# A low-rank mixer on Trainium2: the token mixing from tile 104 on in whole PSUM banks, from a second copy of V

## The chip, the core and the metric

The kernel runs on one core of one Trainium2 chip. Its engines are TensorE (PE in the profile; PEld is its weight loads), VectorE (DVE), ScalarE (ACT), GpSimd (POOL) and SyncE (SP), which issues DMA transfers. The metric is the device time of one execution in microseconds (us). Three runs of the kernel before gave 324.23, 324.48 and 324.81, median 324.48.

## What is computed

```python
def _attn_ref(x, weight):                 # x: (8, 4224, 192), weight: (8, 7)
    w = softmax of weight over its 7 taps
    x_pad = 6 zero rows ahead of x along seq
    out[b, s, head h] = sum_k w[h, k] * x_pad[b, s + k, head h]
    return out                            # a causal convolution, 8 heads of 24

def _moe_ref(x, U, V, w_ch1, w_ch2):      # x is the convolution's result, y below
    xt = x.transpose(0, 2, 1)
    h = xt @ U @ V                        # U: (4224, 32), V: (32, 4224)
    u = x + h.transpose(0, 2, 1)
    ch = np.maximum(u @ w_ch1, 0.0) @ w_ch2   # 192 -> 768 -> 192
    return (u + ch).astype(np.float32)
```

## The kernel before

**Tiles.** A tile is 128 tokens; each of the 8 batches has NT = 33 tiles, 264 in all. Eight tiles make a group, 33 groups. A batch goes through: load of x (four DMA issues on GpSimd's queue, f32 to bf16), GpSimd copies of x shifted by blocks (`x_shift`, six steps), convolution as matmuls with band matrices (`conv32`, L349) evicted by ACT and VectorE into `yt[b]`, then tt = Uᵀy (`tt_mm`, L412; `tt_split`, L426 and L427), the sum of its four partial results with a matrix R (`tt_sum`, L438), which leaves `ttb[b]` with the same 32 rows on all four quarters of the partitions.

**h and u.** `h_tiles(b, j0, j1)` makes h for tiles j0 to j1 of a batch: one matmul for each tile (L469; weights: 32 rows of V by 128 tokens, moving operand: 32 rows of ttb by 192 columns). The PE array is used as four row tiles of 32 rows. Two neighbouring tiles, a pair, share a PSUM bank (384 of its 512 columns), and pair pr uses row tile pr mod 4, so that `V_sb` holds on each quarter of the partitions only the tiles of its pairs. VectorE then adds y to h out of PSUM into the group's buffer `u_sb` (L492), one instruction for a pair, or two where the pair crosses a block of four tiles. A finished group is transposed by a DMA on SP's queue (`transp`, L513, `uT<-u_sb`).

**The channel part.** `w1(g)` (L589) multiplies uT by W1: 36 matmuls of 512 columns, two at a time on two row tiles of 64 rows, with relu evictions by ACT (L603) and VectorE (L605); VectorE takes five of a group's twelve. `w2(g, t0, 2)` (L616) multiplies by W2 for two tiles, 12 matmuls of 192 columns on the whole array; VectorE adds u (L625) and SP's queue stores the result (L633).

**The order** is written out by hand. `SLOTS` lists steps: each has groups for `w1`, then groups for `w2`, and a table that says what is inserted ahead of which of the `w2` pieces (position 0 is ahead of the first, and directly behind W1). Slots 5 to 13 have three groups each: slot k runs groups 3k-9 to 3k-7, so slot 6 runs 9, 10 and 11, and slot 13 the last three. The entries: `c4:0:2:A` is the convolution of batch 4 for 2 heads from head 0 on, with the pattern of engines that evict it; `x5:4` four steps of the shift for batch 5; `t4` tt of batch 4, `s4` its sum; `w105:117` h for tiles 105 to 116 and the transposes of the groups that end there. h runs ahead of W1: in slot 6, tiles 105 to 128 are made while W1 and W2 of tiles 72 to 95 run.

**Buffers.** All PSUM tiles come in turn from one pool of 8 banks, so a matmul that opens a bank waits until the bank of eight allocations before is evicted. `ys` has 3 buffers, `us` 7, `uts` 5, `outs` 8.

**Loads.** `LOADS` ties the four loads of x for a batch to W1's groups: they are held until a named matmul of W1 is done. x of batch 4 is loaded during W1 of groups 6 and 7, in slot 5.

Of the kernel before, what the change touches and what calls it, by code (L numbers as in the profile page):

```python
# [7 lines left out]
ALU = mybir.AluOpType  # L8
ACT = mybir.ActivationFunctionType
BF16 = mybir.dt.bfloat16  # L10
# [4 lines left out]
def kernel(  # L15
# [10 lines left out]
    nc = tc.nc  # L26
    P = nc.NUM_PARTITIONS
    B, S, D = x.shape
# [4 lines left out]
    NT = S // P  # L33
# [3 lines left out]
    NTT = B * NT  # L37
    NG = NTT // GT
    assert NG * GT == NTT
    HB = P // 2  # L40
# [9 lines left out]
    uts = ctx.enter_context(tc.tile_pool(name="uts", bufs=5))  # L50
    rls = ctx.enter_context(tc.tile_pool(name="rls", bufs=3))
    outs = ctx.enter_context(tc.tile_pool(name="outs", bufs=8))
    sml = ctx.enter_context(tc.tile_pool(name="sml", bufs=2))
    psp = ctx.enter_context(tc.tile_pool(name="psp", bufs=8, space=bass.MemoryType.PSUM))

    def bank():
        return psp.tile([P, 512], F32, name="ps", tag="ps")
# [5 lines left out]
    yt = [None] * B  # L63
# [39 lines left out]
    def iota(t, pattern, base, mul):  # L103
# [20 lines left out]
        out=Ur[:, 0:nfull, :], in_=U4[0 : nfull * P, :].rearrange("(k p) c -> p k c", p=P)  # L124
# [10 lines left out]
    for q in range(4):  # L135
        src = moe_V[:, 0 : full * 8 * P].rearrange("r (k q t) -> r k q t", q=4, t=2 * P)
        nc.gpsimd.dma_start(
            out=V_sb[32 * q : 32 * q + 32, 0 : 2 * full, :].rearrange(
                "r (k a) t -> r k (a t)", a=2
            ),  # L140
            in_=src[:, :, q, :],
        )
    W1_sb = cst.tile([P, 3, M4], BF16, name="W1_sb")
    for hf in range(2):
        nc.gpsimd.dma_start(
            out=W1_sb[HB * hf : HB * hf + HB, :, :],
            in_=moe_w_ch1[:, :].rearrange("(c k) m -> k c m", k=HB),
# [6 lines left out]
    for r in range(4):  # L154
        nc.vector.memset(rq[QB * r : QB * r + QB, 0:1], float(QB * r))
    nc.vector.tensor_scalar(
        out=rq[:, 1:2], in0=rq[:, 0:1], scalar1=-4.0, scalar2=None, op0=ALU.mult
# [19 lines left out]
    for hh in range(2):  # L177
# [3 lines left out]
        out=dif[:], in0=dif[:], scalar1=rq[:, 0:1], scalar2=None, op0=ALU.add  # L181
# [5 lines left out]
        out=d_sb[:],  # L187
        in0=w_sb[:],
        in1=mx_sb[:].unsqueeze(2).to_broadcast([P, H, KC]),
        op=ALU.subtract,  # L190
# [5 lines left out]
        out=hot[:],  # L196
        in0=dif[:].unsqueeze(1).to_broadcast([P, KC, BW]),
        in1=tap[:].unsqueeze(2).to_broadcast([P, KC, BW]),
        op=ALU.is_equal,
# [3 lines left out]
        out=ident[:], in0=fp[:], scalar1=float(P), scalar2=None, op0=ALU.is_equal  # L203
# [9 lines left out]
        out=c_sb[:].rearrange("p k h -> p h k"),  # L213
        in0=e_sb[:],
        in1=rs_sb[:].unsqueeze(2).to_broadcast([P, H, KC]),
        op=ALU.mult,
    )
    prs = []
    for hh in range(2):
# [3 lines left out]
            out=pr[:],  # L223
            in0=hot[:].unsqueeze(2).to_broadcast([P, KC, HQ, BW]),
            in1=c_sb[:, :, HQ * hh : HQ * hh + HQ].unsqueeze(3).to_broadcast([P, KC, HQ, BW]),
            op=ALU.mult,
# [5 lines left out]
        out=Eq[:], in0=efp[:], scalar1=rq[:, 1:2], scalar2=None, op0=ALU.is_equal  # L232
# [3 lines left out]
        out=fp[:], in0=fp[:], scalar1=R - 1, scalar2=None, op0=ALU.bitwise_and  # L236
# [3 lines left out]
        out=R4[:], in0=fp[:], scalar1=0.0, scalar2=None, op0=ALU.is_equal  # L240
# [163 lines left out]
    ttb = [[] for _ in range(B)]  # L404
# [46 lines left out]
    def u_group(g):  # L451
        if ut[g] is None:
            ut[g] = us.tile([P, 4, 3, 2, HB], BF16, name="u_sb")
        return ut[g]
# [46 lines left out]
    def h_span(t0, t1):  # L501
        while t0 < t1:
            b = t0 // NT
            te = min(t1, (b + 1) * NT)
            h_tiles(b, t0 - b * NT, te - b * NT)
            t0 = te

    def h_group(g):
        h_span(g * GT, g * GT + GT)

    def transp(g):
        uTt[g] = uts.tile([P, 4, 3, P], BF16, name="uT")
        return nc.sync.dma_start_transpose(  # L513
            out=uTt[g][:].rearrange("p i c t -> p (i c) t"),
            in_=ut[g][:].rearrange("p i c f k -> p (i c f k)"),
        )
# [118 lines left out]
    def held(ins, after):  # L635
        tc.add_manual_dep(
            ins.ins,
            after.ins.name,
            mybir.DependencyInfo(mybir.DependencyClass.Sync, mybir.DependencyReason.DATA),
            reason="transfer held back",  # L640
        )

    def x_load(b, q, after):
        if q == 0:
            x_tile(b)
            x_zero(b, nc.gpsimd)
        held(x_part(b, *XP[q]), after)
# [25 lines left out]
            },  # L673
        ),
    ]
    spans = {
        5: [(80, 88), (88, 96), (96, 105)],
        6: [(105, 117), (117, 129)],
        7: [(129, 140), (140, 152)],
        8: [(152, 164), (164, 175)],  # L680
        9: [(175, 187), (187, 198)],
        10: [(198, 210), (210, 222)],
        11: [(222, 233), (233, 245)],
        12: [(245, 253), (253, 264)],
        13: [],
    }
    for k in range(5, 14):
        gs = list(range(3 * k - 9, 3 * k - 6))
        hs = [f"w{t0}:{t1}" for t0, t1 in spans[k]]
        if k == 5:  # L690
            at = {
                2: ["c3:0:3:AAD"],
                3: ["c3:3:3:AAD"],
                4: ["c3:6:2:A", "x4:4"],
                5: [hs[0]],
                6: ["t3"],
                8: ["s3", hs[1]],
                11: [hs[2]],
            }
        elif k < 10:  # L700
            b = k - 2
            at = {
                0: [f"c{b}:0:2:AAD"],
                2: [f"c{b}:2:3:A"],
                4: [f"c{b}:5:3:AD"] + ([f"x{b + 1}:4"] if b + 1 < B else []),
                5: [hs[0]],
                9: [f"t{b}", hs[1]],
                12: [f"s{b}"],
            }
        elif k < 13:  # L710
            at = {0 if k == 12 else 2: [hs[0]], 5 if k == 12 else 7: [hs[1]]}
        else:
            at = {}
        SLOTS.append((gs, gs, at))

    LOADS = {3: [(4, 1), (4, 4), (5, 1), (5, 4)]}
    for b in range(4, B):
        g = 3 * b - 6
# [26 lines left out]
    for r, (k0, k1) in KP[2].items():  # L745
        j = NB0 // 2 * r + k0
        nc.gpsimd.tensor_copy(
            out=U4_sb[:, o : o + k1 - k0, :, :],
            in_=U_sb[:]
# [8 lines left out]
        out=V_sb[0:32, 2 * (NT // 8), :], in_=moe_V[:, (NT - 1) * P : NT * P]  # L758
# [35 lines left out]
    for r in range(4):  # L794
        q = slice(QB * r, QB * r + QB)
        for hh in range(2):
            nc.gpsimd.tensor_copy(
                out=band2[q, HQ * hh : HQ * hh + HQ, :],
                in_=bands[hh][q, :, HB * (r % 2) : HB * (r % 2) + QB],
            )  # L800

    def do(what):
        if what[0] == "c":
            b, h0, n, engs = what[1:].split(":")
            conv32(int(b), int(h0), int(n), engs)
            return
        if what[0] == "d":
            for h in range(H):
                last = conv(int(what[1:]), h, 1, [0, 1], "AA" if h == 2 else "AD")
            held(transp(3), last)  # L810
            done.append(last)
            return
        if what[0] == "l":
            b, q = (int(v) for v in what[1:].split(":"))
            x_load(b, q, done[-1])
            return
        if what[0] == "x":
            b, n = (int(v) for v in what[1:].split(":"))
            if not steps:
                steps.extend(x_shift(b))  # L820
            for _ in range(n):
                steps.pop(0)()
            return
        if what[0] == "w":
            t0, t1 = (int(v) for v in what[1:].split(":"))
            h_span(t0, t1)
            for g in range(t0 // GT, t1 // GT):
                transp(g)
            return
        n = int(what[1:])  # L830
        if what[0] == "h":
            h_group(n)
            if n > 1 and n != 3:
                transp(n)
        elif what[0] == "t":
            tt_split(n, tt_mm(n, range(NT)))
        else:
            tt_sum(n)

    for gs1, gs2, at in SLOTS:  # L840
        for g in gs1:
            ends = w1(g, RELU0 if g == 1 else RELU)
            for b, blocks in LOADS.items():
                for q, (gb, m) in enumerate(blocks):
                    if gb == g:
                        x_load(b, q, ends[m])
                        if steps:
                            steps.pop(0)()
            if g == 0:
                do("h2")  # L850
        while steps and gs1 != [3]:
            steps.pop(0)()
        npc = 4 * len(gs2)
        for p in range(npc + 1):
            for what in at.get(p, []):
                do(what)
            if p < npc:
                g, k = gs2[p // 4], p % 4
                if g == NG - 1 and k == 3:
                    w2(g, 6, 1)  # L860
                    w2(g, 7, 1)
                else:
                    w2(g, 2 * k, 2)
# [30 lines left out]
```

## Time and profile before

| | |
|---|---|
| median of three runs | 324.48 us |
| the profiled execution | 323.12 us, of which its span is 321.3 us |
| granted TensorE clock | full over the whole span |
| W1, L589: 1188 matmuls | 131.5 us busy |
| W2, L616: 1584 matmuls | 139.8 us busy |
| h, L469: 264 matmuls | 12.0 us busy |
| convolution, L349: 384 matmuls | two groups of 11.8 us busy that lie on each other |
| h + y, L492 on VectorE: 96 of 384 columns, 72 of 192 | 48.4 and 22.4 us busy; 547 and 347 ns each |
| relu, L605 on VectorE: 163 | 105.7 us busy, 688 ns each |
| relu, L603 on ACT: 233 | 124.3 us busy, 604 ns each |
| W2 + u, L625 on VectorE: 131 of 384 columns | 68.8 us busy, 553 ns each |
| DMA queue 1 (stores, transposes) | 38.08 MB, 46.0% of 16 engines' span |
| DMA queue 0 (loads by GpSimd) | 14.60 MB, 39.6% |
| transposes, L513 | 31, from issue to landing 3.2 / 3.8 / 7.9 us (least, median, most) |

A slot of the middle takes 27.8 us. Times of matmuls in the groups are those of one instruction from its start to its modelled end, and they overlap; what a piece of TensorE's work takes is read from the chain of waits, where each row gives start, length, engine, line and count.

### The profile page before, as it was taken

Reading aid. Unit: us, or ns where it says so; the run is one execution under the profiler, and the core shown is the slowest. Engines: PE = TensorE matmul, PEld = TensorE weight load, DVE = VectorE, ACT = ScalarE, POOL = GpSimd, SP = SyncE. Lnnn points to the kernel's source line nnn. Section 1 sums busy time; section 2 is a strip of 40 time slices with the busy share of each in tenths; the row PEclk is TensorE's granted clock in tenths of the full one; section 3 lists DMA queues with packets and bytes.
Section 4 is the critical chain, followed back from the end, with each engine's and each line's share of the span. In section 5 each row is a group of like instructions: output and inputs, shape, how many; then the busy total and the mean of one; then the engine's idle time right before and its main releaser. Section 6 shows DMA issues by size and latency. Waiting matters only on the chain.

```text
span 321.3 us, 9597 instructions
## 1 busy us (share of the span) xinstructions
PE 314.9 (98%) x4004; PEld 218.7 (68%) x4004; DVE 268.7 (84%) x550; ACT 169.5 (53%) x344; POOL 141.6 (44%) x108
## 2 busy tenths in 40 slices
PE   7999999999999999999999999999999999999996
PEld 3757576478677647946864884686597497487495
DVE  6779989987977986996998699699898888897864
ACT  1766723960874396088249609824904903912910
POOL 8763199529947982993798398000000000000000
PEclk9999999999999999999999999999999999999999
DMA  9999993998997999799799963169077079059035
GB/s 105 191 195 169 196 232 101 196 190 253 210 165 147 263 153 194 189 201 154 191 241 139 191 185 111 52 179 218 2 215 228 3 169 275 2 171 272 2 109 188
DMA packets 122443, 53.39 MB, mean 166 GB/s; under 512 B 87712, under 2 KB 122400, under 8 KB 122400
## 3 DMA queue, kind: packets, MB, share of 16 engines
q1 hardware_dynamic: 84528, 38.08, 46.0%
q0 software_dynamic: 37728, 14.60, 39.6%
q8 instruction: 31, 0.51, 0.7%
q14 instruction: 12, 0.10, 0.1%
q10 hardware_dynamic: 144, 0.10, 0.1%
HBM read 29.22 MB, written 25.95 MB: 172 GB/s over the span
## 4 chain that ended last, share of the span: by engine, by line
PE 91%; ACT 3%; DMA 2%; DVE 2%; POOL 1%; issue 1%; POOLq 0%
PE ps L616 42%; PE ps L589 39%; PE ps L349 3%; PE ps L469 3%; DMA x_sb<-in_x_dram 2%; PE ps L412 2%; ACT rl_sb L603 2%; ACT y_sb L266 1%; PE ps L379 1%; POOL x_sb L79 1%; DVE u_sb L492 1%; DVE rl_sb L605 1%; PE ps L438 0%; PE ps L536 0%; DVE out_sb L625 0%
## 5 line engine op out<-in xcount | busy, mean ns | idle before, releaser
L603 ACT ACTIVATE rl_sb<-ps 128x512 bf16<-128x512 f32 x233 | 124.3, 604 | 89.1 <-PE ps L589 77.6
L616 PE MATMUL ps<-W_sb,rl_sb 128*128 128x192 bf16 x1584 | 139.8, 246 | 0.2
L616 PEld LDWEIGHTS <-rl_sb 128*128 128x128 bf16 x1584 | 128.4, 98 | 12.2 <-issue 11.9
L589 PE MATMUL ps<-uT,W_sb 64*128 64x512 bf16 x1188 | 131.5, 376 | 0.3 <-DVE uT L268 0.2
L605 DVE TENSOR_SCALAR rl_sb<-ps 128x512 bf16<-128x512 f32 x163 | 105.7, 688 | 15.2 <-PE ps L589 14.9
L589 PEld LDWEIGHTS <-W_sb 64*128 64x128 bf16 x1188 | 61.3, 94 | 65.9 <-issue 3.0
L625 DVE TENSOR_TENSOR out_sb<-ps,u_sb 128x384 f32<-128x384 f32 (+1 forms) x133 | 69.5, 550 | 25.9 <-PE ps L616 25.0
L315 POOL COPY xb_sb<-x_sb 32x3072 bf16<-32x3072 bf16 (+1 forms) x24 | 67.7, 2820 | 1.1
L492 DVE TENSOR_TENSOR u_sb<-y_sb,ps 128x192 bf16<-128x192 bf16 (+1 forms) x168 | 65.8, 461 | 0.0
L303 POOL COPY xb_sb<-x_sb 128x3072 bf16<-128x3072 bf16 x12 | 32.9, 2742 | 41.5 <-PE ps L349 33.8
L266 ACT ACTIVATE y_sb<-ps 128x408 bf16<-128x408 f32 (+4 forms) x90 | 38.2, 519 | 11.9 <-PE ps L349 9.8
L79 POOL DMA_DIRECT2D x_sb<-in_x_dram x32 | 27.1, 852 | 12.5 <-PE ps L469 7.7
L268 DVE CAST y_sb<-ps 128x408 bf16<-128x408 f32 (+4 forms) x36 | 19.2, 578 | 1.3 <-PE ps L379 1.2
L426 ACT ACTIVATE tt_hi<-ps 128x192 bf16<-128x192 f32 x8 | 2.6, 330 | 27.4 <-PE ps L412 27.4
L469 PE MATMUL ps<-tt_sb,V_sb 32*128 32x192 bf16 x264 | 12.0, 245 | 0.0
L349 PE MATMUL ps<-x_sb,band 64*32 64x384 bf16 x192 | 11.8, 332 | 0.0
L349 PE MATMUL ps<-xb_sb,band 64*32 64x384 bf16 x192 | 11.8, 331 | 0.0
L469 PEld LDWEIGHTS <-V_sb 32*128 32x128 bf16 x264 | 5.8, 92 | 5.7 <-issue 5.5
L379 PE MATMUL ps<-x_sb,band 64*64 64x240 bf16 (+3 forms) x192 | 8.0, 276 | 0.4 <-DMA x_sb<-in_x_dram 0.3
L379 PEld LDWEIGHTS <-band 64*64 64x64 bf16 x192 | 6.0, 106 | 2.2 <-issue 1.5
L349 PEld LDWEIGHTS <-band 64*32 64x32 bf16 x384 | 4.3, 89 | 4.7 <-issue 2.4
L412 PE MATMUL ps<-y_sb,U_sb 128*32 128x192 bf16 x258 | 7.4, 247 | 0.0
(65 smaller groups left out, 66.5 us busy)
## 6 DMA issues: line engine op xcount, KB each, us to landing
out_dram<-out_sb SPq DMA_DIRECT2D x131, 192.0 KB, 3.0
x_sb<-in_x_dram POOLq DMA_DIRECT2D x14, 384.0 KB, 7.2
x_sb<-in_x_dram POOLq DMA_DIRECT2D x7, 432.0 KB, 7.8
x_sb<-in_x_dram POOLq DMA_DIRECT2D x7, 408.0 KB, 7.2
W_sb<-in_moe_w_ch_dram POOLq DMA_DIRECT2D x3, 288.0 KB, 7.5
x_sb<-in_x_dram POOLq DMA_DIRECT2D x1, 504.0 KB, 7.4
uT<-u_sb SPq DMA_TRANSPOSE x31, 3.8
x_sb<-in_x_dram POOLq DMA_DIRECT2D x1, 480.0 KB, 5.6
```

The source lines that it names most:

```text
L79: return nc.gpsimd.dma_start(out=xt[b][HB * r : HB * r + HB, s0:s1, :], in_=x[b, blk * HB : (blk + s1 - s0) * HB, :].rearrange("(j p) d -> ...
L266: nc.scalar.activation(out=out, in_=in_, func=ACT.Copy)
L303: nc.gpsimd.tensor_copy(out=xbt[b][:, s0:s1, :], in_=xt[b][:, s0 + 1 : s1 + 1, :])
L315: nc.gpsimd.tensor_copy(out=xbt[b][q, s0:s1, :], in_=xt[b][q, s0:s1, :])
L349: nc.tensor.matmul(out=pp[r][QB * cg : QB * cg + QB, 0 : nk[r] * GS], lhsT=w[hr], rhs=t[hr, st : st + 2 * nk[r] - 1 : 2, hs], start=True, ...
L469: last = nc.tensor.matmul(out=banks[pr][:, a * D : (a + 1) * D], lhsT=V_sb[32 * q : 32 * q + 32, (j // 8) * 2 + j % 2, :], rhs=ttb[b][32 * ...
L492: nc.vector.tensor_tensor(out=u_group(g)[:, i : i + n, :, hf, :], in0=yt[b][:, run[0] : run[0] + n, :].rearrange("p n (c k) -> p n c k", c=3),
L589: last = nc.tensor.matmul(out=pps[m][hf][:], lhsT=W1_sb[HB * hf : HB * hf + HB, c, m * P : (m + 1) * P], rhs=uTt[g][HB * hf : HB * hf + HB ...
L603: nc.scalar.activation(out=rl[:, m, hf, :], in_=pp[hf][:], func=ACT.Relu)
L605: nc.vector.tensor_scalar_max(out=rl[:, m, hf, :], in0=pp[hf][:], scalar1=0.0)
L616: last = nc.tensor.matmul(out=cps[:, a * D : (a + 1) * D], lhsT=rlt[g][:, m, hf, (i + a) * P : (i + a + 1) * P], rhs=W2_sb[:, m, :], start ...
L625: nc.vector.tensor_tensor(out=o[:, 0:n, :].rearrange("p n (c k) -> p n c k", c=3), in0=cps[:, 0 : n * D].rearrange("p (n c k) -> p n c k", ...
```

## The change

h from tile 104 on is cut in chunks of 64 columns, three to a tile, and eight chunks fill a PSUM bank (512 columns). `h_banks(n)` makes the next n banks, up to four at a time, one on each row tile; a tile that lies across two banks takes two matmuls, with the tile's V as weights in both. Since any row tile may now need any tile of V, `V4_sb` holds all of V on each quarter of the partitions. It is loaded by four issues on GpSimd's queue (`v4_load`) behind W1 of group 7, after the loads of x for batch 4. Its pool stands behind the other large pools, and its rows have 64 unused columns, 896 bytes in all. Tiles below 104 are made as before.

The hand-written order of slots 5 to 12 changes too: h comes as `b4` and `b6` (four and six banks), the convolution's pieces of batches 5 to 7 stand closer together with other engine patterns, and tt and its sum are made at other places: t4 at position 5 of slot 6 and s4 at position 11, t5 in slot 8 between two pieces of the convolution and s5 at position 5, t6 and t7 at position 5 of slot 9.

```diff
+    vs = ctx.enter_context(tc.tile_pool(name="vs", bufs=1))
...
+    TH0 = 104
+    NCH = 3 * TH0
+    VC = 3
+    V4_sb = vs.tile([P, NT // VC, VC * P + HB], BF16, name="V4_sb")
+
+    def v4_load():
+        for q in range(4):
+            nc.gpsimd.dma_start(
+                out=V4_sb[32 * q : 32 * q + 32, :, 0 : VC * P],
+                in_=moe_V[:, :].rearrange("r (j t) -> r j t", t=VC * P),
+            )
+
+    made = [0]
+
+    def h_banks(n):
+
+        c0 = NCH + 8 * made[0]
+        made[0] += n
+        c1 = c0 + 8 * n
+        assert c1 <= 3 * NTT
+        for s0 in range(c0, c1, 32):
+            ps, todo = [], []
+            for k in range(s0, min(s0 + 32, c1), 8):
+                p, q, parts = bank(), len(ps), []
+                for t in range(k // 3, (k + 7) // 3 + 1):
+                    a, e = max(k, 3 * t), min(k + 8, 3 * t + 3)
+                    parts.append((p, q, k, t, a, e))
+                ps.append((p, k))
+                todo.append(parts)
+            for n in range(max(len(parts) for parts in todo)):
+                for parts in todo:
+                    if n >= len(parts):
+                        continue
+                    p, q, k, t, a, e = parts[n]
+                    nc.tensor.matmul(
+                        out=p[:, HB * (a - k) : HB * (e - k)],
+                        lhsT=V4_sb[
+                            32 * q : 32 * q + 32,
+                            t % NT // VC,
+                            t % VC * P : t % VC * P + P,
+                        ],
+                        rhs=ttb[t // NT][
+                            32 * q : 32 * q + 32, HB * (a - 3 * t) : HB * (e - 3 * t)
+                        ],
+                        start=True,
+                        stop=True,
+                        tile_position=(32 * q, 0),
+                    )
+            for p, k in ps:
+                a = k
+                while a < k + 8:
+                    b, blk = a // (3 * NT), a // 12
+                    e = min(k + 8, 12 * (blk + 1), 3 * NT * (b + 1))
+                    y0, i0 = a - 3 * NT * b, a - 12 * blk
+                    nc.vector.tensor_tensor(
+                        out=u_group(blk // 2)[:].rearrange("p i c f k -> p (i c) f k")[
+                            :, i0 : i0 + e - a, blk % 2, :
+                        ],
+                        in0=yt[b][:].rearrange("p j (c k) -> p (j c) k", c=3)[
+                            :, y0 : y0 + e - a, :
+                        ],
+                        in1=p[:, HB * (a - k) : HB * (e - k)].rearrange(
+                            "p (n k) -> p n k", k=HB
+                        ),
+                        op=ALU.add,
+                    )
+                    a = e
+        for g in range(c0 // 24, c1 // 24):
+            transp(g)
+
...
-    spans = {
-        5: [(80, 88), (88, 96), (96, 105)],
-        6: [(105, 117), (117, 129)],
...
-        12: [(245, 253), (253, 264)],
-        13: [],
+    late_slots = {
+        5: "2:c3:0:3:AAD 3:c3:3:3:AAD 4:c3:6:2:A 4:x4:4 5:w80:88 6:t3 8:s3 8:w88:96 11:w96:104",
+        6: "0:c4:0:2:A 2:c4:2:3:AAD 4:c4:5:3:AAD 4:x5:4 5:b4 5:t4 8:b4 11:s4",
+        7: "0:c5:0:2:AD 1:c5:2:3:AAD 3:c5:5:3:AAD 3:x6:4 4:b4 7:b4",
+        8: "0:c6:0:2:AD 0:t5 0:c6:2:3:A 4:c6:5:3:AAAD 4:x7:4 5:s5 5:b4 9:b4",
+        9: "0:c7:0:2:AD 1:c7:2:3:AD 2:c7:5:3:AAAD 3:b4 5:t6 5:t7 5:b6 9:s6 12:s7",
+        10: "0:b4 9:b4",
+        11: "0:b4 6:b6",
+        12: "0:b4 10:b4",
+        13: "",
     }
     for k in range(5, 14):
         gs = list(range(3 * k - 9, 3 * k - 6))
...
-        elif k < 10:
-            b = k - 2
-            at = {
-                0: [f"c{b}:0:2:AAD"],
-                2: [f"c{b}:2:3:A"],
-                4: [f"c{b}:5:3:AD"] + ([f"x{b + 1}:4"] if b + 1 < B else []),
-                5: [hs[0]],
-                9: [f"t{b}", hs[1]],
-                12: [f"s{b}"],
-            }
-        elif k < 13:
-            at = {0 if k == 12 else 2: [hs[0]], 5 if k == 12 else 7: [hs[1]]}
-        else:
-            at = {}
+        at = {}
+        for item in late_slots[k].split():
+            p, what = item.split(":", 1)
+            at.setdefault(int(p), []).append(what)
         SLOTS.append((gs, gs, at))
...
+        if what[0] == "b":
+            h_banks(int(what[1:]))
+            return
...
             if g == 0:
                 do("h2")
+            if g == 7:
+                v4_load()
```

More of the change, by code (lines that the diff above doesn't have):

```diff
@@ L675 @@
     ]
-    spans = {
-        5: [(80, 88), (88, 96), (96, 105)],
-        6: [(105, 117), (117, 129)],
[L679 to L683, printed above, removed]
-        12: [(245, 253), (253, 264)],
-        13: [],
+    late_slots = {
[8 more added lines that the diff above has]
+        13: "",
     }
@@ L688 @@
         gs = list(range(3 * k - 9, 3 * k - 6))
-        hs = [f"w{t0}:{t1}" for t0, t1 in spans[k]]
-        if k == 5:
-            at = {
-                2: ["c3:0:3:AAD"],
-                3: ["c3:3:3:AAD"],
-                4: ["c3:6:2:A", "x4:4"],
-                5: [hs[0]],
-                6: ["t3"],
-                8: ["s3", hs[1]],
-                11: [hs[2]],
-            }
-        elif k < 10:
-            b = k - 2
-            at = {
-                0: [f"c{b}:0:2:AAD"],
-                2: [f"c{b}:2:3:A"],
-                4: [f"c{b}:5:3:AD"] + ([f"x{b + 1}:4"] if b + 1 < B else []),
-                5: [hs[0]],
-                9: [f"t{b}", hs[1]],
-                12: [f"s{b}"],
-            }
-        elif k < 13:
-            at = {0 if k == 12 else 2: [hs[0]], 5 if k == 12 else 7: [hs[1]]}
-        else:
-            at = {}
+        at = {}
+        for item in late_slots[k].split():
+            p, what = item.split(":", 1)
+            at.setdefault(int(p), []).append(what)
         SLOTS.append((gs, gs, at))
```

## The prediction

> **What bounds the kernel now.** I read the page's busy shares, then the chain of waits in order of time, then the groups by line with shapes kept apart, then timelines of VectorE, GpSimd and the queues at the places that the change moves.
>
> ```profile
> PE 314.9 (98%) x4004; PEld 218.7 (68%) x4004; DVE 268.7 (84%) x550; ACT 169.5 (53%) x344; POOL 141.6 (44%) x108
> PE 91%; ACT 3%; DMA 2%; DVE 2%; POOL 1%; issue 1%; POOLq 0%
> ```
>
> TensorE is busy for 98% of the span and the chain lies on it for 91%. Slot 7 and the end of the run in that chain (start, length, engine, line, count):
>
> ```profile
> 151.57 2.09 PE ps L616 x24
> 153.66 0.64 PE ps L349 x19
> 154.30 1.09 PE ps L616 x12
> 155.40 0.43 PE ps L469 x11
> 155.83 4.07 PE ps L616 x48
> 159.90 0.85 PE ps L412 x33
> 160.74 0.43 PE ps L469 x12
> 161.18 3.08 PE ps L616 x36
> 164.25 0.17 PE ps L438 x2
> 164.42 11.76 PE ps L589 x108
> ...
> 258.78 0.52 PE ps L469 x11
> ...
> 264.79 5.06 PE ps L616 x60
> 269.84 11.76 PE ps L589 x108
> 281.60 0.28 PE ps L469 x8
> ```
>
> From 67 us to 318 us no other engine stands in the chain: TensorE goes from piece to piece at one rhythm. So a change after slot 5 saves only what it takes out of TensorE's own sequence, and costs what makes TensorE wait. Two prices follow from these rows. Twelve L616 matmuls take 0.99 where the same shape follows (`4.07` is 48 of them) and 1.09 to 1.10 ahead of another shape: **a boundary between tile shapes costs 0.10**. And an h insert (L469) of 8 tiles, which gives each of the four row tiles two matmuls, takes 0.28; 12 tiles give the fullest row tile four and take 0.43; a badly aligned 11 gives one five and takes 0.52. So **a round costs 0.08 and an insert 0.11 besides**.
>
> **The h matmuls.** h already runs on four row tiles; what changes is the filling. Before, pair pr goes to row tile pr mod 4, so 12 tiles load two row tiles with 4 matmuls and two with 2. After, four banks of eight 64-column chunks give every row tile 512 columns, in three or four matmuls issued round by round: three rounds with a 192-column matmul in each, and a fourth with 64 columns. Such an insert is 0.11 + 3 x 0.08 + 0.03 = 0.38 (64 columns at a third of 0.08). The two six-bank inserts add a second set on two row tiles, 0.20 more: 0.58. There are 14 inserts before (6.04 in the chain's rows from slot 6 on) and 14 after: 12 x 0.38 + 2 x 0.58 = 5.72. That is **-0.3**. The trace shows no matmul of 64 columns on 32 rows. Bounds: filled without any loss, 512 columns take 0.21 and the sum is 12 x 0.32 + 2 x 0.54 = 4.9 (-1.1); if each of the 200 matmuls (160 before) takes a whole round, it is 12 x 0.43 + 2 x 0.75 = 6.7 (+0.6). I take 0.38, since L589 with 512 columns (two at a time, 11.76 / 54 = 0.218) and L616 with 192 (0.083) lie on a line with almost no fixed part.
>
> The Trainium skill (TensorEngine Tiling (Array Packing), Performance Considerations, on instruction overhead) gives each matmul some 60 cycles of overhead and advises against splitting a dimension that is already small. The rows above show no such addition at 192 columns (0.083 for 192 columns and 0.218 for 512 leave 0.002 that does not grow with the columns); by that rule as an addition the smaller pieces would lose what the filling gains.
>
> **The regrouped inserts.** Counting changes of tile shape in the issue order from slot 6 to slot 12: 12 in each of slots 6 to 9, 6, 6 and 5 before, 65 in all; after 12, 11, 11, 12, 5, 5, 5, or 61. The gain comes from c6 and t5 standing together at position 0 of slot 8, and from b4 moved to position 0, beside W1, in slots 10 and 11. 4 x 0.10 is **-0.4** (0 if a boundary hides elsewhere). The R matmuls (L438, shape of L616) cost no boundary where they stand alone, before and after.
>
> **tt of batch 4, made earlier.** t4 now stands at position 5 of slot 6, straight behind b4. From the start of conv's last piece to it lie 0.64 + 1.10 + 0.38 = 2.1. It needs the whole y. ACT begins 0.42 after such a piece (154.01 for 153.59 on the timeline) and took three evictions in 1.25; the pattern AAD gives it four, so it ends at 0.42 + 1.25 + 0.4 = 2.1. I put **+0.1** on it (0 to +0.4); TensorE takes its work in order, so all of the slot behind t4 moves by as much. t5, t6, t7 stand far behind their evictions.
>
> **VectorE.** The adds of 14 inserts, 55 of 384 and 49 of 192 columns, become 83: 38 of 512, 39 of 256, six odd ones. Back to back a 384-column add costs 0.464 (four in 1.94, one 0.547):
>
> ```profile
> 104.62 1.94 DVE L492 TENSOR_TENSOR u_sb<-y_sb,ps 128x384 bf16<-128x384 bf16 x4
> 106.47 1.48 DVE L625 TENSOR_TENSOR out_sb<-ps,u_sb 128x384 f32<-128x384 f32 x3
> 107.87 2.33 DVE L492 TENSOR_TENSOR u_sb<-y_sb,ps 128x384 bf16<-128x384 bf16 x7
> 110.12 0.55 DVE L625 TENSOR_TENSOR out_sb<-ps,u_sb 128x384 f32<-128x384 f32 x1
> 110.59 4.27 DVE L605 TENSOR_SCALAR rl_sb<-ps 128x512 bf16<-128x512 f32 x7
> ```
>
> A 192-column one is 0.264, and on the line through both 512 is 0.60 and 256 is 0.33: 38.5 before, 37.3 after. Three convolution evictions move from ACT to VectorE (+1.5). VectorE's sum stays, and nothing is saved there, because TensorE does not wait for it. These rows show how near it is, though: slot 6's W1 starts at 108.74 by TensorE and the first relu on VectorE only at 110.59; W1's fifth pair of banks needs that relu, at 108.74 + 4 x 0.65 = 111.3, and it ends at 111.27. After, slot 5's last span has one tile less, which gives 0.3 to 0.5 of room there, and the nearest places become slot 8 and slot 12, whose second insert comes late (positions 9 and 10). In slot 12, T being b4's start, the adds run from T + 0.6 (as at 287.45 for 286.87 before) to 3.0, the two L625 behind them to 4.0; the first relu ends at 4.6, and the fifth pair needs it at T + 0.38 + 2 x 1.0 + 0.1 + 2.6 = 5.1. In slot 8 three W2 pieces lie between, and the room is larger. No wait, then, with 0.4 to spare.
>
> **The transposes on SP's queue.** What W1 of group 31 waits for at the end of slot 12 is its transpose: first bank added by T + 1.3, issued at T + 1.4, and 3.8 us (median of 31 from issue to landing; 3.2 to 7.9) to land: 5.2. W1 of group 31 starts at T + 2.5 + 3.9 = 6.4. Room 1.2. Groups 19 (slot 8) and 25 (slot 10) have 1 us more. The stores queued behind these transposes on SP have eight buffers, and W1 follows, which makes none.
>
> **V's second load.** Four issues on GpSimd's queue behind x's batch 4. V_sb's issues took about 0.6 each, so 2.4, in a gap that is there:
>
> ```profile
> 89.98 1.68 POOL L79 DMA_DIRECT2D x_sb<-in_x_dram  x2
> 98.58 2.74 POOL L303 COPY xb_sb<-x_sb 128x3072 bf16<-128x3072 bf16 x1 [6.92 <-PE ps L349]
> ```
>
> Without the gap, GpSimd's copies would be 2.4 later; they end at 118.0 (3.06 from 114.89) and the convolution starts at 120.5, so even that fits. The load writes 4 x 270 KB. Queue 0 moved 14.60 MB in 39.6% of 321.3 us, 8.7 us per MB: 9.4 us at most of all engines, from about 94 on, where the DMA share is 1.45 before 96 and 0.8 to 0.9 from 96 to 104. It can hold up stores (eight buffers, the first one is wanted again 12 us later) and the transpose of group 10, issued at 102.0, landing near 107 and wanted at 112.7; only beyond 5 us of delay would each further one be TensorE's. V itself is wanted at 127. **0**, with +1 as the far end. Rows and place of the buffer: no instruction here shows a price, 0.
>
> **Sum.** -0.3 - 0.4 + 0.1 = -0.6. The profiled execution took 323.12 (span 321.3, 1.8 around it), so 322.5 for such a one; the median of the runs shown is 1.36 above it, so **323.9**.
>
> **Rivals.** *(1) The pieces cost by their number.* A matmul of 64 columns takes a round: +0.6 - 0.4 + 0.1 = +0.3, 324.8. For: 40 more weight loads, and W2's 83 ns also carry one each. Against: rounds overlap weight loads with matmuls on other row tiles. The skill's overhead rule named above points here; the rows at 192 and 512 columns do not. *(2) Late adds hold W1 back, slower.* In slots 8, 10 and 12 the second insert stands at position 9 or 10, so VectorE comes to the relus late or the transpose does. It decides once VectorE is over 0.4 behind my count or a transpose takes over 5 us. A transpose as slow as the slowest seen, 7.9, would stop slot 13 by 7.9 + 1.4 - 6.4 = 2.9; typically I count 0.7 in each of three slots: 2.1 - 0.6 = +1.5, 326.0. For: the room of 0.0 in slot 6 now, and 5 us transposes late in the run. Against: x's loads, beside which the slow ones fell, have ended by 182. *(3) It does nothing measurable:* the boundaries stay, the inserts give 0.3, the waits take it: 324.3. *(4) The filling is lossless* and boundaries go: -1.1 - 0.4 = -1.5, 323.0.
>
> **Chances.** Forecast (323.6 to 324.1) 0.50, (1) 0.10, (2) 0.16, (3) 0.16, (4) 0.08. About 0.2%, 0.65 us, is what a measurement of this kernel tells from no change, and my forecast lies next to that line: of its 0.50 I give 0.32 to faster. Faster: 0.32 + 0.08 and 0.02 of (3) = 0.42. Slower: 0.16 and most of (1) = 0.24. Same: 0.34. The range reaches from (4) to near (2): 323.0 to 325.6.
>
> **What would show it.** h inserts of 0.38 with 13 or 14 matmuls in the chain; W1 still 11.76 in slots 6 to 13; no VectorE or DMA row in the chain after 67 us; t4 with a gap of at most 0.4. Wrong: inserts of 0.43 or more (1), a W1 longer than 11.8 or a transpose ahead of it in the chain (2).

## The result and the profile after

The first timing gave 321.82 us (median of five runs, 321.71 to 322.09) against 324.48 for the kernel before (five runs, 323.15 to 325.14): ratio 0.992, interval 0.990 to 0.995. Timed again on one chip with more runs it is 322.69 (ten runs) against 323.44 (33 runs): ratio **0.996, interval 0.995 to 0.998**. So the kernel became faster, by about 0.4%; the 323.9 of the prediction lay too high, and both medians are below its range of 323.0 to 325.6.

The profiled execution took 321.84, of which its span is 320.0 (before: 323.12 and 321.3). Its busy shares, the head of its chain of waits, and from that chain slot 7 and the last inserts (start, length, engine, line, count; L687 is W2, L660 W1, L350 the convolution, L543 the new h):

```profile
PE 314.5 (98%) x4044; PEld 218.9 (68%) x4044; DVE 269.3 (84%) x531; ACT 168.2 (53%) x341; POOL 144.0 (45%) x112
PE 91%; ACT 4%; DMA 2%; DVE 2%; issue 0%; POOL 0%; POOLq 0%
```

```profile
150.48 2.09 PE ps L687 x24
152.56 0.64 PE ps L350 x19
153.21 1.10 PE ps L687 x12
154.30 0.33 PE ps L543 x10
154.63 3.08 PE ps L687 x36
157.71 0.33 PE ps L543 x10
158.04 5.06 PE ps L687 x60
163.10 11.76 PE ps L660 x108
...
261.98 0.55 PE ps L543 x16
262.53 6.05 PE ps L687 x72
268.57 11.76 PE ps L660 x108
280.33 0.34 PE ps L543 x10
```

The reader is to see three things. W1 and W2 cost what they did before: 11.76, and 1.10 for twelve W2 matmuls behind another shape. An insert of four banks takes 0.33 where 12 tiles took 0.43, one of six banks 0.55. And from 67 us on no other engine stands between TensorE's rows. From the start of W1 in slot 6 to that in slot 13, TensorE took 185.59 us before (108.74 to 294.33) and 184.26 after (108.77 to 293.03). This number recurs below: it is the same to 0.01 in every profile of the same order, while the rest of the span is not.

VectorE on the two edges that the prediction looked at, slot 6 and slot 13 (L493 and L563 add y to the old and the new h, L696 adds u to W2's result, L676 is the relu):

```profile
107.90 2.06 DVE L493 TENSOR_TENSOR u_sb<-y_sb,ps 128x384 bf16<-128x384 bf16 x6
109.88 0.55 DVE L696 TENSOR_TENSOR out_sb<-ps,u_sb 128x384 f32<-128x384 f32 x1
110.35 4.53 DVE L676 TENSOR_SCALAR rl_sb<-ps 128x512 bf16<-128x512 f32 x7
...
291.19 2.54 DVE L563 TENSOR_TENSOR u_sb<-y_sb,ps 128x512 bf16<-128x512 bf16 x5
293.64 1.02 DVE L696 TENSOR_TENSOR out_sb<-ps,u_sb 128x384 f32<-128x384 f32 x2
294.57 4.59 DVE L676 TENSOR_SCALAR rl_sb<-ps 128x512 bf16<-128x512 f32 x7
```

The first relu of slot 6 starts 0.24 earlier than before (110.35 for 110.59). In slot 13 it starts 3.96 after b4 (290.61 to 294.57), as counted, and TensorE does not wait.

### The profile page after: what moved, and what is told of

Its sections match the earlier page's. It is cut to its first block, busy times and chain, and to the rows that moved or that the text cites. A ratio compares the mean times of both kernels' runs of the same rounds, so it can differ in the third digit from the quotient of the medians.

```text
span 320.0 us, 9664 instructions
## 1 busy us (share of the span) xinstructions
PE 314.5 (98%) x4044; PEld 218.9 (68%) x4044; DVE 269.3 (84%) x531; ACT 168.2 (53%) x341; POOL 144.0 (45%) x112
## 4 chain that ended last, share of the span: by engine, by line
PE 91%; ACT 4%; DMA 2%; DVE 2%; issue 0%; POOL 0%; POOLq 0%
PE ps L687 42%; PE ps L660 39%; PE ps L350 3%; DMA x_sb<-in_x_dram 2%; PE ps L413 2%; ACT rl_sb L674 2%; ACT y_sb L267 2%; PE ps L543 2%; PE ps L380 1%; PE ps L470 1%; DVE u_sb L493 1%; DVE rl_sb L676 1%; PE ps L439 0%; PE ps L607 0%; POOL x_sb L80 0%
## 5 line engine op out<-in xcount | busy, mean ns | idle before, releaser
L687 PE MATMUL ps<-W_sb,rl_sb 128*128 128x192 bf16 x1584 | 139.6, 246 | 0.2
L687 PEld LDWEIGHTS <-rl_sb 128*128 128x128 bf16 x1584 | 128.6, 98 | 10.4 <-issue 8.7
L660 PE MATMUL ps<-uT,W_sb 64*128 64x512 bf16 x1188 | 131.5, 376 | 0.3 <-DVE uT L269 0.2
L676 DVE TENSOR_SCALAR rl_sb<-ps 128x512 bf16<-128x512 f32 x163 | 106.1, 688 | 16.5 <-PE ps L660 15.9
L660 PEld LDWEIGHTS <-W_sb 64*128 64x128 bf16 x1188 | 61.2, 94 | 66.1 <-issue 3.4
L696 DVE TENSOR_TENSOR out_sb<-ps,u_sb 128x384 f32<-128x384 f32 (+1 forms) x133 | 69.5, 549 | 23.6 <-PE ps L687 22.9
L267 ACT ACTIVATE y_sb<-ps 128x384 bf16<-128x384 f32 (+4 forms) x87 | 37.0, 518 | 13.2 <-PE ps L350 11.0
L563 DVE TENSOR_TENSOR u_sb<-y_sb,ps 128x512 bf16<-128x512 bf16 (+3 forms) x83 | 38.5, 532 | 0.0
L493 DVE TENSOR_TENSOR u_sb<-y_sb,ps 128x384 bf16<-128x384 bf16 (+1 forms) x63 | 25.9, 476 | 0.0
L269 DVE CAST y_sb<-ps 128x408 bf16<-128x408 f32 (+4 forms) x39 | 20.8, 578 | 1.5 <-PE ps L380 1.3
L350 PE MATMUL ps<-x_sb,band 64*32 64x384 bf16 x192 | 11.8, 332 | 0.0
L350 PE MATMUL ps<-xb_sb,band 64*32 64x384 bf16 x192 | 11.8, 332 | 0.0
L164 PE MATMUL ps<-zz 128*128 128x512 f32 (+1 forms) x10 | 7.0, 851 | 1.1 <-DVE zz L152 1.1
L350 PEld LDWEIGHTS <-band 64*32 64x32 bf16 x384 | 4.2, 90 | 4.7 <-issue 2.4
```

The source lines that it names most:

```text
L267: nc.scalar.activation(out=out, in_=in_, func=ACT.Copy)
L350: nc.tensor.matmul(out=pp[r][QB * cg : QB * cg + QB, 0 : nk[r] * GS], lhsT=w[hr], rhs=t[hr, st : st + 2 * nk[r] - 1 : 2, hs], start=True, ...
L493: nc.vector.tensor_tensor(out=u_group(g)[:, i : i + n, :, hf, :], in0=yt[b][:, run[0] : run[0] + n, :].rearrange("p n (c k) -> p n c k", c=3),
L563: nc.vector.tensor_tensor(out=u_group(blk // 2)[:].rearrange("p i c f k -> p (i c) f k")[:, i0 : i0 + e - a, blk % 2, :], in0=yt[b][:].rea ...
L660: last = nc.tensor.matmul(out=pps[m][hf][:], lhsT=W1_sb[HB * hf : HB * hf + HB, c, m * P : (m + 1) * P], rhs=uTt[g][HB * hf : HB * hf + HB ...
L676: nc.vector.tensor_scalar_max(out=rl[:, m, hf, :], in0=pp[hf][:], scalar1=0.0)
```

## The experiments

"Sum" is the time from W1 of slot 6 to W1 of slot 13.

**The kernel before, once more.** No edit.

> The kernel before, unchanged, run and profiled once more. Its profiled execution of record took 323.12 us, below the median of its timed runs (324.48, five runs from 323.15 to 325.14), while the changed kernel's profiled execution (321.84) stands at the median of its own (321.82, 321.71 to 322.09). Theory A (hidden waits): the kernel before has waits in most executions that its profile of record did not show; then a new profile has a span over 322 us with gaps in TensorE's sequence after 67 us that add up to the difference, most likely in W1 at the start of slot 6, where VectorE's first relu had no room. Theory B (baseline scatter): the span is 321.3 again or the added time lies outside TensorE's sequence after 67 us (in the head before 67 us, or behind the last matmul). Ratio 1.00 by either.

Median 323.52 (11 runs) beside 323.39 (29 runs, 322.88 to 325.44): ratio 1.002, interval 0.999 to 1.004. The usual execution of the kernel before is near 323.3, with a tail up to 325. The profile caught a late one (324.04, span 322.3). Its sum is 185.59, so nothing was hidden there: theory A falls. The lateness lies ahead of slot 6: W1 of slot 5 begins at 80.80 instead of 80.44, and slot 5 takes 28.86 instead of 28.30. VectorE on that execution's timeline:

```profile
77.65 0.56 DVE L625 TENSOR_TENSOR out_sb<-ps,u_sb 128x384 f32<-128x384 f32 x1 [1.31 <-DMA out_dram<-out_sb]
78.13 2.00 DVE L492 TENSOR_TENSOR u_sb<-y_sb,ps 128x192 bf16<-128x192 bf16 x5
80.05 1.02 DVE L625 TENSOR_TENSOR out_sb<-ps,u_sb 128x384 f32<-128x384 f32 x2
80.98 1.94 DVE L492 TENSOR_TENSOR u_sb<-y_sb,ps 128x384 bf16<-128x384 bf16 x4
82.83 0.55 DVE L625 TENSOR_TENSOR out_sb<-ps,u_sb 128x384 f32<-128x384 f32 x1
83.30 4.27 DVE L605 TENSOR_SCALAR rl_sb<-ps 128x512 bf16<-128x512 f32 x7
```

VectorE waits 1.31 us for a store to free its buffer, and comes to the relus at 83.30, where W1 of group 6 had begun at 80.80: that group takes 4.33 instead of 3.89. The last load of x for batch 3, under way at the same time, landed at 76.65 in this execution and at 73.56 in the other.

**The new h at the old places**, twice. The second time slot 9 has six banks at position 5 and four at 9.

```diff
 from the changed kernel:
-        7: "0:c5:0:2:AD 1:c5:2:3:AAD 3:c5:5:3:AAD 3:x6:4 4:b4 7:b4",
+        7: "0:c5:0:2:AAD 2:c5:2:3:A 4:c5:5:3:AD 4:x6:4 5:b4 9:t5 9:b4 12:s5",
...
+        9: "0:c7:0:2:AAD 2:c7:2:3:A 4:c7:5:3:AD 5:b4 9:t7 9:b6 12:s7",
 the second time:
+        9: "0:c7:0:2:AAD 2:c7:2:3:A 4:c7:5:3:AD 5:b6 9:t7 9:b4 12:s7",
```

> The new h (whole banks, V4_sb and its load) at the old positions: the convolution, tt and the sums stand as before, h at the positions of the old spans. If the saving is in the inserts (6.13 us by their starts before, 5.17 after), the profiled span is 320.3 to 320.5, 0.95 below 321.3. If the regrouping carried it, 321.2. In the timed runs theory A gives about 322.2 (hidden waits gone with the shorter last insert of slot 5), theory B 323.5.

> The new h at the old positions as in the first such run, but in slot 9 six banks at position 5 and four at position 9 instead of four and six. The 0.27 us that W1 of group 21 lost there came from adds of six banks late in the slot. If so it goes, and the sum of slots 6 to 12 is 184.80: 0.79 below 185.59 by the inserts alone, which leaves 0.54 to the regrouping. If the loss stays, it is the transposes that are late.

The first: sum 185.07, median 323.27, ratio 1.000 (0.998 to 1.002), the profile with a late head. W1 of slot 10 had lost 0.46 in all; the 0.27 that I had read was one group's share. The second: sum **184.61** (184.80 was expected), no loss in slot 10, median 322.36 in eight runs, ratio 0.997 (0.995 to 1.000). So the inserts alone are worth 0.98, and six banks at position 9 cost 0.46 of it. Why, from VectorE's timeline of the first:

```profile
216.78 3.80 DVE L563 TENSOR_TENSOR u_sb<-y_sb,ps 128x256 bf16<-128x256 bf16 x8
220.49 1.48 DVE L696 TENSOR_TENSOR out_sb<-ps,u_sb 128x384 f32<-128x384 f32 x3
221.89 0.35 DVE L433 CAST tt_sb<-ps 128x192 bf16<-128x192 f32 x1
222.15 4.27 DVE L676 TENSOR_SCALAR rl_sb<-ps 128x512 bf16<-128x512 f32 x7
```

Eight adds keep VectorE until 220.6; its first relu starts 2.3 after W1 did (219.82), back to back with the next six, and ends at 222.8, later than W1's fifth pair of banks wants it (219.82 + 2.6). This is the mechanism that the prediction had put against the change. It is real, and the change's own order stays clear of it.

**The old h at the new places.**

```diff
 from the changed kernel, without V4_sb and its load:
-        9: "0:c7:0:2:AD 1:c7:2:3:AD 2:c7:5:3:AAAD 3:b4 5:t6 5:t7 5:b6 9:s6 12:s7",
+        9: "0:c7:0:2:AD 1:c7:2:3:AD 2:c7:5:3:AAAD 3:w168:179 5:t6 5:t7 5:w179:195 9:s6 12:s7",
```

> The old h (pairs, V_sb, no second load) at the new positions, in spans rounded to whole tiles (104:115, 115:126, 126:136 and so on). Four boundaries of 0.095 less: span 320.9 if nothing waits; the insert of 16 tiles in slot 9 may wait for banks (0.3 more). In the timed runs theory A gives 322.7 if the hidden waits hung on slot 5's last insert (8 tiles here too), theory B 324.1.

Slower: median 327.86, ratio 1.014 (1.013 to 1.016), sum 189.74. The expectation missed what pairs cost in banks: 11 tiles of an odd batch open six banks, 16 tiles eight, all of them before one is free. TensorE in slot 9:

```profile
213.29 0.50 PE L469 MATMUL ps<-tt_sb,V_sb 32*128 32x192 bf16 x7
214.23 0.40 PE L469 MATMUL ps<-tt_sb,V_sb 32*128 32x192 bf16 x9 [0.44 <-DVE tt_lo L427]
215.20 1.99 PE L686 MATMUL ps<-W_sb,rl_sb 128*128 128x192 bf16 x22 [0.57 <-DVE u_sb L492]
```

The insert waits for VectorE to empty the bank of tt, and W2 behind it for the first add. Here it costs 1.9 us where six whole banks take 0.55. All 14 inserts, each from its start to that of the next piece, take 10.71 instead of 6.13, which is more than the whole loss; the rest of the regrouping still gains 0.44. The regrouped order is worth 0.35 with whole banks (184.61 to 184.26) and loses 4.15 with pairs in these spans (185.59 to 189.74).

**The second load alone**, in the kernel before, with V4_sb, its pool and `v4_load` as in the change and nothing that reads it. Of the edit, the call:

```diff
+            if g == 7:
+                v4_load()
```

> The kernel before with the second load of V and its buffer added, which nothing reads. If the load and the buffer's place cost nothing, the span is 321.3 and the ratio 1.000 (within 0.2%). If the load holds up stores or transposes, slot 6 starts later than 108.7 and the ratio is over 1.002. If the shifted place of the small buffers behind it is what made the changed kernel steadier, the ratio is about 0.996.

Ratio 1.000 (0.999 to 1.001), sum 185.59: it costs nothing that can be measured. It is not free of effect: the transpose of group 10 landed at 110.1 here and at 110.9 in the changed kernel, before at 107.0, and it is wanted at 112.7 (112.8 here). Of the 5.7 us of room the changed kernel has 1.8 left.

**The changed kernel once more, and more store buffers.**

```diff
-    outs = ctx.enter_context(tc.tile_pool(name="outs", bufs=8))
+    outs = ctx.enter_context(tc.tile_pool(name="outs", bufs=12))
```

> The changed kernel timed again beside the kernel before on one chip. The profiles say that TensorE's sequence from W1 of slot 6 to W1 of slot 13 is 185.59 us before, in three profiles, and 184.26 after. Theory B (baseline scatter): the true gain is these 1.33 us, ratio 0.9955 to 0.9965, and the first five timed runs of the kernel before (median 324.48) had caught more of its late executions than its usual 323.3; the changed kernel has such late executions too, up to +1 or +2 us, in some of ten runs. Theory A (the change also removed hidden waits): ratio about 0.992 again, and the changed kernel's runs keep within 0.4 us.

> The kernel before with 12 store buffers in place of 8. In the second profile of the kernel before, VectorE waited 1.31 us for a store buffer in slot 4, beside the loads of x for batch 3, came late to W1 of group 6, and TensorE lost 0.44 us there and 0.12 further on. If this is what makes the late executions, 12 buffers take them away: no wait of L625 on a store after 60 us, W1 of group 6 at 3.89, runs within 0.5 us of each other at 322.8 to 323.3. If the loads hold up something else (transposes), the scatter stays.

> The changed kernel with 12 store buffers. By the same reasoning its usual execution stays at 321.8 (slots 6 to 12 sum to 184.26) and late ones vanish, so it is the best of all: 321.5 to 321.8. If the place of the buffers behind matters, it is slower than the changed kernel.

The changed kernel: median 322.69, ratio 0.996 as above, ten runs from 321.79 to 323.52. Theory B stands. The new profile is a late execution too (322.74), with a sum of 184.26 and, in slots 4 and 5, the same event as in the kernel before, this time with the store in the chain itself:

```profile
70.93 7.12 DMA out_dram<-out_sb
...
82.94 0.47 DVE out_sb L696
83.41 0.61 DVE rl_sb L676
...
84.06 9.22 PE ps L660 x83
```

With 12 buffers the kernel before had median 323.44, ratio 1.000 (0.998 to 1.002), and the changed kernel 321.88, ratio **0.995 (0.993 to 0.996)**, sum 184.26. In neither profile does VectorE wait for a store in slots 4 and 5. But both caught usual executions (323.28 and 321.96), and so did the first profiles with eight buffers (323.12 and 321.84), which have no such wait there either; these profiles do not show, then, that the buffers took it away. A few late runs stayed in both (up to 326.66 and 323.74), so the runs of the kernel before did not keep within 0.5 us of each other, as was expected if the buffers were all of it.

**Row tiles in another order.** A set's matmuls are issued bank by bank.

```diff
-            for n in range(max(len(parts) for parts in todo)):
-                for parts in todo:
-                    if n >= len(parts):
-                        continue
-                    p, q, k, t, a, e = parts[n]
+            for parts in todo:
+                for p, q, k, t, a, e in parts:
```

> The changed kernel with the matmuls of a set issued bank by bank (all of the first row tile's, then all of the second's) instead of round by round. The inserts took 0.333 us, not the 0.38 counted by rounds. If TensorE starts matmuls in program order and a row tile holds only its own, bank by bank leaves no overlap except at the seams: an insert is up to 0.11 + 4 x 0.2 = 0.9 us, and slots 6 to 12 sum to some 8 us more than 184.26. If row tiles run free of the order, it stays at 184.26 and the gain over 0.38 is such freedom.

In one execution the sum is 184.52, 0.26 more, and three of the inserts in its chain read:

```profile
154.29 0.34 PE ps L540 x10
...
182.81 0.36 PE ps L540 x9
...
262.15 0.56 PE ps L540 x14
```

Not 0.9. TensorE's groups for this line at the head of the first of these inserts, with the shapes kept apart, from 154.20 to 154.24 us (shapes, count, then busy us and mean ns; V_sb is V4_sb here, the view leaves numbers out):

```profile
L540 PE MATMUL ps<-tt_sb,V_sb 32*128 32x192 bf16 x1 | 0.3, 251 | 0.0
L540 PE MATMUL ps<-tt_sb,V_sb 32*128 32x128 bf16 x1 | 0.2, 225 | 0.0
L540 PE MATMUL ps<-tt_sb,V_sb 32*128 32x64 bf16 x1 | 0.2, 198 | 0.0
```

Three matmuls have started, of 128, 192 and 64 columns. In program order this insert's columns are 128, 192, 192 for the first row tile, 192, 192, 128 for the second, then 64, 192, 192, 64 for the third: the one of 64 is the seventh at the earliest, and it has started ahead of at least four of the six before it. The fourth row tile's first follows at once; all four first matmuls start within 0.033 us. So a row tile takes its next matmul when it is free itself, whatever an earlier one in the program waits for.

**Rows and place of V4_sb.** Rows without the 64 columns; its pool ahead of the others; and the first of these with 12 store buffers.

```diff
-    V4_sb = vs.tile([P, NT // VC, VC * P + HB], BF16, name="V4_sb")
+    V4_sb = vs.tile([P, NT // VC, VC * P], BF16, name="V4_sb")
 or
+    vs = ctx.enter_context(tc.tile_pool(name="vs", bufs=1))
     xs = ctx.enter_context(tc.tile_pool(name="xs", bufs=2))
```

> The changed kernel with V4_sb's rows of 768 bytes, without the 64 unused columns. If the padding only places bytes, slots 6 to 12 sum to 184.26 and the median is the changed kernel's (321.8 to 322.7). If it keeps the load's packets apart, the packets of queue 0 become fewer and larger, and the transposes of groups 10 and 11 (landed 4 us later than before in the changed kernel) move. If it matters for the time, the ratio is over 0.998.

> The changed kernel with V4_sb's pool ahead of the large pools, so that all of these lie 9,856 bytes further on each partition. If the place does not matter, slots 6 to 12 sum to 184.26 and the median lies between 321.8 and 322.7. If the addresses of the large buffers set how fast transfers or engines run, either the pieces lengthen (W1 over 11.76, adds over 0.60) or late executions become the rule, and the ratio rises to 1.000 or over.

> The changed kernel with 12 store buffers and V4_sb's rows of 768 bytes. With eight buffers 6 of 10, 4 of 12 and 5 of 12 runs of the changed order were above 322.6; with 12 it was 2 of 12. If the wait for a store buffer in slot 4 makes most of the late executions, again at most 3 of some 12 runs lie above 322.6 and the median is 321.7 to 321.9. If that was chance, 4 to 6 do and the median is 322.1 to 322.7. Slots 6 to 12 sum to 184.26 by either.

Neither padding nor place shows in TensorE's sequence: 184.26 both times. Medians 322.34 and 322.11, ratio 0.997 for both (0.995 to 0.998). The padding does shape the load:

```profile
q0 software_dynamic: 39200, 15.68, 43.5%
```

```profile
q0 software_dynamic: 37920, 15.68, 41.3%
```

First the changed kernel, then the one with tight rows (packets, MB, share of 16 engines): 1,280 packets fewer for the same bytes. That this moves the transposes is not shown: group 10's landed at 108.7 with tight rows, but at 109.7 in the profile with tight rows and 12 buffers, and with padding at 110.9 the first time and 109.3 the second.

The profile with V4_sb's pool in front is a late execution (323.21), and late from another place than the two above. From its chain, slots 3 and 4:

```profile
40.69 7.40 DMA uT<-u_sb
48.09 0.05 issue
48.14 4.06 PE ps L660 x36
...
57.07 1.87 PE ps L660 x14
58.94 7.92 DMA uT<-u_sb
```

TensorE waits for transposes here. That of group 3 lands at 48.09, in the first profile of the changed kernel at 44.97, and W1 of group 3 starts at 48.14 instead of 46.52. VectorE waits for no store in this execution, and slot 5 takes its usual 28.30.

Tight rows with 12 buffers gave 322.06 (seven runs, 321.82 to 322.53), ratio 0.995 (0.993 to 0.997): none of seven above 322.6, where eight buffers had 6 of 10, 4 of 12 and 5 of 12 (one of them the outlier of 328.5) in these sessions, none of five in the first, and 12 buffers with padding 2 of 12. The median is in neither range expected. That store buffers make most of the late executions is suggested by these counts and not shown; the late execution with the pool in front came from another wait.

## Why the prediction was wrong

**The frame held.** TensorE's sequence sets the time. Boundaries cost 0.10 and W1 and W2 did not move. (The prediction puts the 0.10 on a piece ahead of another shape; in the rows it falls on the piece behind one, which changes no sum.) The regrouping was put at -0.4 and the wait of t4 at +0.1; together they measured -0.35, with 0.08 for the wait (b4 ahead of t4 takes 0.41 instead of 0.33), so four boundaries gave 0.43. The second load was put at 0 and cost 0, with its four issues 2.46 us for 2.4. The late adds had about the room that was counted. The transposes had less: the prediction counted 1.2 us for group 31 and 1 more for group 19, and in the changed kernel they landed 0.88 and 0.64 ahead of their W1 (group 25, counted like group 19, had 2.85). With 12 store buffers group 31's landed 0.05 ahead, and W1 of slot 13 took 11.82 instead of 11.76. Rival (2) was nearer than the text says.

**The h inserts were mis-sized.** The step said "three rounds with a 192-column matmul in each, and a fourth with 64 columns" and took 0.38 and 0.58, a gain of 0.3. The runs show 0.33 and 0.55: by TensorE's starts all 14 take 5.17 instead of 6.13, a gain of 0.96, and the isolating run has 0.98. The rounds were the error. Row tiles do not wait for each other, so an insert is 0.11 to 0.12 and what the fullest row tile has to stream: 512 columns here, 768 in most of the old inserts. By TensorE's starts the old inserts take 0.28, 0.43 to 0.45 and 0.51 for 384, 768 and 960 columns and the new ones, but for the one that holds t4's wait, 0.33 and 0.55 for 512 and 1,024: all within 0.02 of one line. The old ones alone fit both readings, because there every matmul had 192 columns. The lower bound in the text, "filled without any loss", 0.32 and 0.54, was within 0.02 of the right value, and rival (4) with its -1.5 was right in mechanism: measured -1.33.

**The base was the second error.** "The median of the runs shown is 1.36 above it" took three runs for the kernel's level. The usual execution before is at 323.3, where the profiled one (323.12) nearly is; those three had come from the tail. With the true -1.33 the forecast from the profiled execution is 321.8, what was measured first. From the median it would have been 323.1, still 1.3 too high. That all five of the first runs of the changed kernel were usual executions was luck: in the next session six of ten were late, and the median was 322.69.

On the Trainium skill's rule of some 60 cycles for each matmul (TensorEngine Tiling (Array Packing), Performance Considerations): no run here shows it as an addition. The same page of the Trainium skill says under Key Properties that tiles work independently of each other. With this the bank-by-bank run agrees: 0.36 where 0.9 was estimated for program order. TensorE: Matmul & The Clock Gate (Part 3, The mechanism), also of the Trainium skill, has matmuls start and end strictly in program order. Here the starts in the trace differ between row tiles, the seventh matmul being the third to start, and the measurement decides; of the ends, which are modelled, the trace can say nothing.

## What to carry to other kernels

Where row tiles share TensorE, count the columns of the fullest one; cutting operands into smaller matmuls to level them cost no more than 0.01 us an insert here, down to 64 columns, and filling whole PSUM banks also saves banks. The old pairs, with more banks to an insert, lost 4.15 in the tighter order. A regrouping and the piece that makes room for it must be judged together: one gained 0.98 alone, the other lost 4.15 alone, and both gained 1.33. Compare a part of the trace that repeats exactly, not the whole time, when the kernel's own executions scatter by more than the change.

## What was not expected of the hardware

Matmuls of different row tiles overtake each other in the order of their starts. The kernel, changed or not, has executions 1 to 2 us late (about a quarter of 85 runs of the kernel before were over 323.9). Two late profiles show VectorE waiting for a store buffer in slots 4 and 5, while the loads of a batch are under way and land late too; a third shows TensorE waiting for a transpose in slots 3 and 4 and no wait for a store. What holds these transfers up is open. The changed kernel with 12 buffers (321.88, ratio 0.995) led the change alone (322.69) in the one session that had both; the change alone had 321.82 in its first five runs, so that the buffers help is not shown.
